# The last columns of one record of each round, loaded in sixteen strided pieces

## The chip, the core and the metric

The kernel runs on one core of a Trainium2 chip. The metric is the time of one execution on the device in microseconds. The kernel before took 724.65 us in the median of three runs (724.24 to 724.74).

The core has a matrix engine (TensorE, PE in the profile), a vector engine (DVE), a scalar engine (ACT), a general engine (POOL, unused here) and a queue that issues transfers (SP). Sixteen DMA engines move the bytes between the chip's memory and the core's SBUF, whose 128 partitions are the rows of every tile below.

## The reference

A decode step of two attention layers and two feed-forward layers, in float32, with one new token for each of 4 sequences:

```
x = x + A(layernorm(x))      # attention, 32 heads of 128, the last 1024 cached positions
x = x + B(layernorm(x))      # relu(x @ w1) @ w2, 640 -> 1728 -> 640
x = x + A(layernorm(x))      # the same weights and caches again
x = x + B(layernorm(x))
```

In `A`, the queries are `x @ wq`; the scores of each head against its own 1024 cached keys go through a softmax; the weighted sum of the cached values goes through `wo`. Every key, value and weight is used for four tokens at most, so the work is nearly all reading: each of the two passes over the attention reads the whole cache.

## The kernel before

The host packs everything that one head needs into a record of 128 rows and 9472 columns (`REC`): the head's part of `wq` in columns 0 to 640, its keys for four sequences up to column 4736 (`V`), its values up to 8832 (`WO`), and its part of `wo` in the last 640. A record is 4736 KB. There are 32, and SBUF holds five at a time, in `slot0` to `slot4`; a further tile, `ring`, holds feed-forward weights and, for a while, parts of records.

There are two rounds, each of 32 records and one feed-forward layer. Round 0 takes the records in the order 0 to 31. Round 1 starts with records 27 to 31, which still lie in the slots, and goes on with 0 to 26 (`order`). So position 20 is record 20 in round 0, which lies in slot 0, and record 15 in round 1, which lies in slot 1.

For one head, PE computes the query (tile `q_ps`), transposes it (`misc`), computes the scores (`sc_ps`), transposes the weights of the softmax (`pt_ps`), sums the values (`o_ps`), transposes the result (`misc`) and adds its projection to `acc`. The heads are interleaved: within one step of the loop, PE takes the scores of record n+1, then the values of record n, then the query of record n+2, then the output projection of record n. The last of these releases the slot of record n.

All loads of records and weights are issued by SP, in one order that is fixed when the program is built: `items` lists them, and `pump` issues the head of the list once its columns of its buffer are no longer in use (`live`, cut down by `done`). On the chip, SP takes the loads strictly in that order. A load whose semaphores aren't there yet holds up all that stand behind it. It waits for PE where it overwrites columns that PE reads.

The completion of a load is told by a semaphore. The program uses eight for the loads (named DMAHW0 to DMAHW7 in the instruction list), in turn: each load takes the next one, and one that takes a semaphore waits first until the load that had it before, eight issues earlier, has landed.

Most records are one load of 128 rows by 9472 columns. The first record, the last three of each round (`ending`), and the records that enter while round 1 begins are cut into pieces. All instructions come out of one helper, so nearly all rows of the profile say L81; the tiles tell them apart.

Of the kernel before, what the change touches and what calls it, by code (L numbers as in the profile page):

```python
# [35 lines left out]
P = 128  # L36
# [8 lines left out]
REC = 2 * D + 8 * W  # L45
# [13 lines left out]
W1_SLOT = [[0, 1], [2], [3], [4]]  # L59
W2_SLOT = [22, 20, 8, 4]  # L60
LATE = 3


IDENT, MEAN, NCON = 0, 128, 256
# [24 lines left out]
def decode_kernel(ctx: ExitStack, tc: tile.TileContext, xf, cst, rec, w1, w2, out):  # L89
    nc = tc.nc  # L90
    pe, dve, act, sp = (InOrder(tc, e) for e in (nc.tensor, nc.vector, nc.scalar, nc.sync))
# [13 lines left out]
    hT = on[:, FD:FD + 4 * NB * B].rearrange("p (t j b) -> p t j b", t=4, j=NB)  # L105
    oTs = sb.tile([P, LATE, B], F32, name="oTs")
    qs = sb.tile([P, DH], F32, name="qs")
# [22 lines left out]
    order = [list(range(H)), list(range(H - NS, H)) + list(range(H - NS))]  # L130
    LAST = H - NS

    def home(h, r):

        return h % NS if not r or h >= LAST else (h - 6 + LAST) % NS

    items = []
    at = {}
    live = []
    buffers = dict(enumerate(slot)) | {"ring": ring}  # L140

    def load(key, src, lo, hi, buf, col):
        items.append((key, src, lo, hi, buf, col))

    def piece(r, h, lo, hi, buf=None, col=None):
        load(("rec", r, h), rec[h], lo, hi, home(h, r) if buf is None else buf, lo if col is None else col)

    def ending(r, hs, late):
        a, b, c = hs[-3:]
        end = WO if late else REC  # L150
        for h, lo, hi in ((a, 0, V), (b, 0, V), (a, V, end), (c, 0, V), (b, V, end), (c, V, V + VH), (c, V + VH, end)):
            piece(r, h, lo, hi)
        if late:
            for h in hs[-3:]:
                piece(r, h, WO, REC)


    hs = order[0]
    piece(0, hs[0], 0, V)
    piece(0, hs[0], V, REC)  # L160
    for h in hs[1:-3]:
        piece(0, h, 0, REC)
    ending(0, hs, True)
    for k, col in enumerate(W1_RING):
        load(("w1", 0), w1, k * FF, k * FF + FF, "ring", col)
    n = 0
    for size, col in W2_RING:
        load(("w2", 0), w2, n * FD, (n + size) * FD, "ring", col)
        n += size
# [13 lines left out]
        piece(1, new[i], 0, V, *((old[i], 0) if i < 5 else ("ring", 0)))  # L183
        piece(1, new[i], V, REC, old[i - 1], V)
    for h in new[6:-3]:
        piece(1, h, 0, REC)
    ending(1, hs, False)
    for blocks in W1_SLOT:
        load(("w1", 1), w1, blocks[0] * FF, (blocks[-1] + 1) * FF, home(LAST + 1, 0), blocks[0] * FF)
# [5 lines left out]
    def pump():  # L195

        while items:
            key, src, lo, hi, buf, col = items[0]
            if any(b == buf and x < col + hi - lo and col < y for b, x, y in live):
                return  # L200
            sp.dma_start(buffers[buf][:, col:col + hi - lo], src[:, lo:hi])
            live.append((buf, col, col + hi - lo))
            at.setdefault(key, []).append((lo, hi, buf, col))
            items.pop(0)
# [11 lines left out]
    def done(key, lo, hi):  # L216

        if key[0] == "rec" and key[1] == 0 and key[2] >= LAST:
            return
        for x, y, buf, col in pieces(key):  # L220
            a, b = col + max(lo, x) - x, col + min(hi, y) - x
            if a < b:
                rest = []
                for bb, u, v in live:
                    if bb != buf or v <= a or b <= u:
                        rest.append((bb, u, v))
                    else:
                        rest += [(bb, p, q) for p, q in ((u, a), (b, v)) if p < q]
                live[:] = rest
        pump()  # L230
# [6 lines left out]
    def center(fill):  # L237

        x = acc[:, :FD]
        dve.tensor_reduce(sums, x, op=OP.add, axis=AX.X)  # L240
        if fill:
            busy(256)
        pe.matmul(misc[:, 0:1], mean_of, sums, start=True, stop=True)
        if fill:
            busy(512)
            busy(256)
        dve.tensor_scalar(xc, x, misc[:, 0:1], None, op0=OP.subtract)
        dve.transpose(xT, xc)
        act.activation(square, xc, AF.Square, accum_out=squares)
        dve.tensor_copy(x_sb, x)  # L250
# [117 lines left out]


    pump()  # L370
    residual()
    for r in range(2):
        hs = order[r]
        late = LATE if r == 0 else 1
        center(r > 0)
# [79 lines left out]
```

## Time and profile before

| | before |
|---|---|
| median of 3 runs | 724.65 us |
| the profiled execution's own time | 724.7 us |
| its span, first to last instruction | 722.9 us |
| bytes moved, mean rate over the span | 304.74 MB, 422 GB/s |
| DMA engines' time taken by the loads' queue (q1) | 98.6% |
| PE busy | 530.8 us, 73% |
| DVE busy | 206.5 us, 29% |
| ACT busy | 90.3 us, 12% |

The page shows the span in 40 slices of 18 us, with the DMA engines' mean busy share in tenths and the rate in GB/s in each. The chain of waits is followed back from the last instruction: each row has its start, its length, and the engine or the transfer that it stood in. A row "DMA slot<-rec" in it is a transfer from its issue to its landing, the time behind earlier transfers included. SPq is the queue that issues the loads; its rows give the time of the issue alone, and its waits are listed apart. In the views by windows, the columns are the stretch, its length, the busy time and number of instructions of PE, weight loads, DVE, ACT and POOL, the granted clock of PE, the busy share of the DMA engines (a packet counted whole where it starts, so it can pass 1) and GB/s.

### The profile page before, as it was taken

Reading aid. Unit: us, or ns where it says so; the run is one execution under the profiler, and the core shown is the slowest. Engines: PE = TensorE matmul, PEld = TensorE weight load, DVE = VectorE, ACT = ScalarE, POOL = GpSimd, SP = SyncE. Lnnn points to the kernel's source line nnn. Section 1 sums busy time; section 2 is a strip of 40 time slices with the busy share of each in tenths; the row PEclk is TensorE's granted clock in tenths of the full one; section 3 lists DMA queues with packets and bytes.
Section 4 is the critical chain, followed back from the end, with each engine's and each line's share of the span. In section 5 each row is a group of like instructions: output and inputs, shape, how many; then the busy total and the mean of one; then the engine's idle time right before and its main releaser. Section 6 shows DMA issues by size and latency. Waiting matters only on the chain.

```text
span 722.9 us, 9922 instructions
## 1 busy us (share of the span) xinstructions
PE 530.8 (73%) x4420; PEld 220.2 (30%) x4420; DVE 206.5 (29%) x541; ACT 90.3 (12%) x154; POOL 0.2 (0%) x4
## 2 busy tenths in 40 slices
PE   0666867668677686868999889776867768586987
PEld 0232322323233232323323333232322323232332
DVE  1222233232232223323421343422223222222430
ACT  0301011010110101101111221201011010101120
POOL 0000000000000000000000000000000000000000
PEclk9978788687787878778999999978788788778999
DMA  9999999999999999999999999999999999999996
GB/s 381 436 435 433 429 432 422 429 431 435 436 433 431 429 429 423 433 435 420 421 401 371 410 426 428 446 431 424 429 432 433 433 433 432 433 431 416 429 419 255
DMA packets 15161, 304.74 MB, mean 422 GB/s; under 512 B 1680, under 2 KB 2064, under 8 KB 5136
## 3 DMA queue, kind: packets, MB, share of 16 engines
q1 hardware_dynamic: 14832, 303.91, 98.6%
q8 instruction: 34, 0.56, 0.3%
q10 hardware_dynamic: 288, 0.21, 0.1%
q14 instruction: 7, 0.06, 0.0%
HBM read 304.04 MB, written 0.08 MB: 421 GB/s over the span
## 4 chain that ended last, share of the span: by engine, by line
DMA 81%; PE 15%; DVE 2%; issue 1%; ACT 0%; SPq 0%; DVEq 0%; ACTq 0%
DMA slot<-rec 76%; DMA slot<-w 3%; PE sc_ps L81 3%; PE misc L81 3%; PE acc L81 3%; PE o_ps L81 3%; DMA ring<-w 2%; PE q_ps L81 2%; PE pt_ps L81 2%; DVE on L81 1%; DVE oTs L81 1%; DVE small L81 0%; ACT prob L81 0%; SPq L81 0%; SPq L78 0%
## 5 line engine op out<-in xcount | busy, mean ns | idle before, releaser
L81 PE MATMUL q_ps<-slot,xT 128*4 128x128 f32 x620 | 46.9, 318 | 138.3 <-DMA slot<-rec 137.3
L81 ACT ACTIVATE prob<-sc_ps,small 128x1024 f32<-128x1024 f32 x64 | 71.3, 1115 | 563.0 <-DVE small L81 555.4
L81 PE MATMUL sc_ps<-slot,qT 128*4 128x512 f32 x992 | 132.7, 657 | 1.8 <-DVE qT L81 1.0
L81 PE MATMUL o_ps<-slot,pT 128*4 128x512 f32 x1014 | 120.5, 592 | 1.8 <-DVE pT L81 0.9
L81 DVE TENSOR_REDUCE small<-sc_ps 128x1 f32<-128x1024 f32 x64 | 78.4, 1225 | 129.4 <-PE sc_ps L81 129.4
L81 PE MATMUL pt_ps<-con,prob 128*128 128x128 f32 x518 | 113.4, 364 | 0.0
L81 PEld LDWEIGHTS pt_ps<-con,prob 128*128 128x128 f32 x518 | 83.9, 189 | 28.3 <-issue 27.4
L81 PEld LDWEIGHTS q_ps<-slot,xT 128*4 128x4 f32 x620 | 20.8, 88 | 193.8 <-DMA slot<-rec 181.3
L81 PE MATMUL misc<-con,on 128*128 128x128 f32 x256 | 54.6, 350 | 9.9 <-DVE on L81 9.9
L81 DVE TENSOR_SCALAR qs<-q_ps,small 128x128 f32<-128x128 f32 x64 | 22.3, 349 | 138.3 <-PE q_ps L81 138.0
L81 DVE COPY pT<-pt_ps 128x16 f32<-128x16 f32 x128 | 22.1, 174 | 123.1 <-PE pt_ps L81 123.1
L81 DVE TENSOR_SCALAR on<-o_ps,small 128x512 f32<-128x512 f32 x64 | 48.0, 751 | 29.2 <-PE o_ps L81 29.2
L81 PEld LDWEIGHTS o_ps<-slot,pT 128*4 128x4 f32 x1014 | 25.5, 87 | 82.8 <-issue 76.4
L81 PE MATMUL acc<-slot,oTs 128*4 128x160 f32 x512 | 38.2, 382 | 16.3 <-DVE oTs L81 16.3
L81 PEld LDWEIGHTS misc<-con,on 128*128 128x128 f32 x256 | 34.6, 171 | 31.9 <-DVE on L81 17.4
L81 PEld LDWEIGHTS sc_ps<-slot,qT 128*4 128x4 f32 x992 | 20.8, 89 | 70.5 <-issue 64.8
L81 PE MATMUL misc<-con,qs 128*128 128x128 f32 x64 | 23.5, 368 | 2.3 <-DVE qs L81 2.1
L81 PE MATMUL sc_ps<-slot,con 128*1 128x512 f32 (+1 forms) x50 | 20.8, 506 | 0.0
L81 DVE TENSOR_REDUCE oTs<-misc 128x4 f32<-128x16 f32 x64 | 11.2, 175 | 33.5 <-PE misc L81 33.5
L81 PEld LDWEIGHTS acc<-slot,oTs 128*4 128x4 f32 x512 | 7.2, 84 | 36.6 <-DVE oTs L81 35.8
L81 DVE TENSOR_REDUCE qT<-misc 128x16 f32<-128x64 f32 x64 | 14.4, 225 | 3.4 <-PE misc L81 2.0
L81 PEld LDWEIGHTS misc<-con,qs 128*128 128x128 f32 x64 | 12.6, 198 | 4.1 <-ACT small L81 2.2
(45 smaller groups left out, 101.7 us busy)
## 6 DMA issues: line engine op xcount, KB each, us to landing
slot<-rec SPq DMA_DIRECT2D x46, 4736.0 KB, 31.1
slot<-rec SPq DMA_DIRECT2D x17, 2368.0 KB, 22.1
slot<-rec SPq DMA_DIRECT2D x5, 1024.0 KB, 31.9
ring<-w SPq DMA_DIRECT2D x5, 864.0 KB, 13.7
slot<-rec SPq DMA_DIRECT2D x2, 2048.0 KB, 41.9
slot<-rec SPq DMA_DIRECT2D x3, 1344.0 KB, 9.0
slot<-w SPq DMA_DIRECT2D x3, 864.0 KB, 31.0
ring<-rec SPq DMA_DIRECT2D x1, 2368.0 KB, 16.2
```

The costliest lines, as they stand in the source:

```text
L81: r = build(*args, **kwargs)
```

## The change

One whole record in each round, at position 20, is loaded in two parts: columns 0 to 8320 in one load of 128 rows as before, and the last 1152 columns (the last 512 of the values and all of the `wo` part) in 16 loads. Load r of the 16 takes the 8 rows r, r+16, r+32 up to r+112, from and to the same rows, so that each moves 8 x 4608 bytes, 36 KB. `pump` issues all 16 one behind the other; they count as one piece for the kernel's own bookkeeping, but each is a load of its own with its own semaphore. The bytes and where they land are the same, and so is the work of the other engines. SP issues 32 loads more.

```diff
+EVEN = [slice(0, P)]
+UNEVEN = [slice(r, P, 16) for r in range(16)]
+SHIFTED = 20
+STRIP = 1152
...
-    def piece(r, h, lo, hi, buf=None, col=None):
-        load(("rec", r, h), rec[h], lo, hi, home(h, r) if buf is None else buf, lo if col is None else col)
+    def piece(r, h, lo, hi, buf=None, col=None, rows=EVEN):
+        load(("rec", r, h), rec[h], lo, hi, home(h, r) if buf is None else buf, lo if col is None else col, rows)
+
+    def whole(r, h):
+        if h == order[r][SHIFTED]:
+            piece(r, h, 0, REC - STRIP)
+            piece(r, h, REC - STRIP, REC, rows=UNEVEN)
+        else:
+            piece(r, h, 0, REC)
...
     for h in hs[1:-3]:
-        piece(0, h, 0, REC)
+        whole(0, h)
...
     for h in new[6:-3]:
-        piece(1, h, 0, REC)
+        whole(1, h)
...
-            key, src, lo, hi, buf, col = items[0]
+            key, src, lo, hi, buf, col, rows = items[0]
...
-            sp.dma_start(buffers[buf][:, col:col + hi - lo], src[:, lo:hi])
+            for p in rows:
+                sp.dma_start(buffers[buf][p, col:col + hi - lo], src[p, lo:hi])
```

More of the change, by code (lines that the diff above doesn't have):

```diff
@@ L140, in decode_kernel, with load @@
     buffers = dict(enumerate(slot)) | {"ring": ring}
-    def load(key, src, lo, hi, buf, col):
-        items.append((key, src, lo, hi, buf, col))
-    def piece(r, h, lo, hi, buf=None, col=None):
-        load(("rec", r, h), rec[h], lo, hi, home(h, r) if buf is None else buf, lo if col is None else col)
+    def load(key, src, lo, hi, buf, col, rows=EVEN):
+        items.append((key, src, lo, hi, buf, col, rows))
+    def piece(r, h, lo, hi, buf=None, col=None, rows=EVEN):
[6 more added lines that the diff above has]
+            piece(r, h, 0, REC)
     def ending(r, hs, late):
```

## The prediction

> **What bounds the kernel now.** I read the page first: the DMA lines, then the chain that ended last.
>
> ```profile
> span 722.9 us, 9922 instructions
> DMA  9999999999999999999999999999999999999996
> GB/s 381 436 435 433 429 432 422 429 431 435 436 433 431 429 429 423 433 435 420 421 401 371 410 426 428 446 431 424 429 432 433 433 433 432 433 431 416 429 419 255
> ...
> DMA 81%; PE 15%; DVE 2%; issue 1%; ACT 0%; SPq 0%; DVEq 0%; ACTq 0%
> ...
> slot<-rec SPq DMA_DIRECT2D x46, 4736.0 KB, 31.1
> ```
>
> All 16 DMA engines are nine tenths busy or more from the first slice to the last but one, and the chain is transfers for 81% of the span. The 46 whole records land 31.1 us (median) after they are issued. The chain of waits in order of time gives the pace around the two places that the change touches:
>
> ```profile
> 176.91 30.69 DMA slot<-rec
> 207.65 0.60 PE q_ps L81 x10
> ...
> 210.23 31.98 DMA slot<-rec
> 242.25 0.84 PE q_ps L81 x10
> ...
> 276.01 0.60 PE q_ps L81 x10
> ...
> 309.65 0.60 PE q_ps L81 x10
> ...
> 550.68 0.60 PE q_ps L81 x10
> ...
> 552.65 31.64 DMA slot<-rec
> 584.34 1.01 PE q_ps L81 x10
> ```
>
> Each row of q_ps is the query of a record that has just landed, and the chain shows every third record. 242.25 to 309.65 is six records, 11.23 us each; 550.68 to 584.34 is three, 11.22 us each. So a record is issued nearly three records ahead of its landing: itself and about two more are queued. The transfer issued at 210.23 is record 20 of round 0, the first that is split: counting three records per step from the start, it follows the release of record 15's slot and lands at 242.2. Of round 1, position 20 is record 15, one before the record issued at 552.65 and landed at 584.3, so it lands near 573.1. Both stand where nothing but the transfers sets the pace, as the windows say:
>
> ```profile
> 200.00:300.00 100.00, 71.67 (x557) 29.76 (x559) 27.82 (x70) 10.85 (x18) 0.00 (x0) 0.80 1.00 430
> 550.00:650.00 100.00, 70.91 (x559) 30.70 (x563) 26.32 (x70) 9.64 (x16) 0.00 (x0) 0.80 1.00 431
> ```
>
> The last columns are the DMA share, 1.00, and GB/s, 430 and 431, or 27 GB/s for one of 16 engines; PE is busy for 72 and 71 us of 100. Time in which the DMA engines have nothing queued is therefore lost for good, and time on PE is not.
>
> **What SP waits for.** The DMA queue's own waits, over the run and then from 328 to 350 us:
>
> ```profile
> SPq L81 <- PE acc L81: 499.0, 52, 26.6
> SPq L81 <- DMA slot<-rec: 68.2, 17, 6.0
> ...
> SPq L81 <- DMA slot<-rec: 16.6, 4, 5.3
> ```
>
> Mostly SP waits for PE to release a slot. But it has also waited 17 times for a landing. These come where round 0's ending is cut in many short loads: a load takes one of eight completion semaphores in turn, and before it is issued, the load eight issues earlier must have landed. With whole records, the load eight back is long done. In the changed kernel's instruction list for SP, the first split record reads (semaphore waited for in brackets):
>
> ```
> L86 DMACopy slot0_70<-rec 128x8320 [waits DMAHW2_49,PE_49]
> L86 DMACopy slot0_70<-rec 8x1152 [waits PE_49]
> L86 DMACopy slot0_70<-rec 8x1152 x2
> L86 DMACopy slot0_70<-rec 8x1152 [waits DMAHW3_49]
> ...
> L86 DMACopy slot0_70<-rec 8x1152 [waits DMAHW7_49]
> L86 DMACopy slot0_70<-rec 8x1152 [waits DMAHW0_49]
> ...
> L86 DMACopy slot0_70<-rec 8x1152 [waits DMAHW7_49]
> L86 DMACopy slot1_71<-rec 128x9472 [waits DMAHW0_49,PE_49]
> ```
>
> Number the sixteen short loads 0 to 15. Loads 0 to 2 go out at once; 3 to 6 wait for records 16 to 19; load 7 waits for the landing of the 8320 columns of its own record; 8 to 15 wait for loads 0 to 7, and record 21 waits for load 8. The same order stands at round 1's split record.
>
> **The change part by part.**
>
> *The shortened load.* 8320 of 9472 columns take 11.24 x 8320/9472 = 9.87 us, so it lands 1.37 us earlier, at about 240.9 us. It needs the slot only up to the first three quarters of the last values, so it can be issued a few us earlier; that is worth nothing, as two records are queued ahead of it.
>
> *The sixteen loads, up to load 7.* Load 7 can't be issued before 240.9, and record 21, which went out about 222 us before (one record after 210.23), is stuck behind it for some 20 us. By then records 18, 19 and the 8320 columns have drained: the queue is empty but for loads 0 to 6, one row of 4608 B to an engine, 4608/27 = 0.17 us each and 1.2 us together. That is a stall of the whole stream, and this is the term that decides. From the last byte of the 8320 columns to full rate on record 21:
>
> ```profile
> 720.44 0.35 SPq L81 DMA_DIRECT2D out<-on  x1
> ...
> out<-on SPq DMA_DIRECT2D x1, 80.0 KB, 1.6
> ```
> ```profile
> 721.25:721.50 0.25, 0.00 (x0) 0.00 (x0) 0.00 (x0) 0.00 (x0) 0.00 (x0) 1.00 0.71 210
> 721.50:721.75 0.25, 0.00 (x0) 0.00 (x0) 0.00 (x0) 0.00 (x0) 0.00 (x0) 1.00 0.41 118
> 721.75:722.00 0.25, 0.00 (x0) 0.00 (x0) 0.00 (x0) 0.00 (x0) 0.00 (x0) 1.00 0.00 0
> ```
>
> 1. Landing: the store of the output is issued at 720.44 and done 1.6 us later, at 722.04; its last bytes move between 721.50 and 721.75. From last byte to semaphore is 0.3 to 0.5 us: 0.4.
>
> ```profile
> 1.16 0.90 SPq L81 DMA_DIRECT2D slot<-rec  x2
> ...
> 1.16 2.73 SPq L81 DMA_DIRECT2D slot<-rec  x5
> ...
> 300.40 0.80 SPq L81 DMA_DIRECT2D slot<-rec  x2
> ...
> 395.53 0.33 SPq L81 DMA_DIRECT2D slot<-rec  x1
> ```
>
> 2. Issues: loads 7 to 15 are nine issues ahead of record 21. SP's rows show loads issued one behind the other: two in 0.80 and 0.90 us, five in 2.73, so 0.40 to 0.55 us each, and 0.33 is one alone. No load of 8 rows is in the trace. The spread is small and nothing in the rows ties the time to a load's size; I take 0.43, so 9 x 0.43 = 3.9 us. The ends: at 0.33 it is 3.0, at 0.55 it is 5.0. Were a short load's issue free, load 15 still waits for load 7's landing, a trip of 1.6 us by the store, and then 1.6 + 0.33 = 1.9.
>
> ```profile
> 395.50:396.00 0.50, 0.50 (x8) 0.00 (x0) 0.00 (x0) 0.00 (x0) 0.00 (x0) 1.00 0.53 221
> 396.00:396.25 0.25, 0.25 (x4) 0.00 (x0) 0.00 (x0) 0.00 (x0) 0.00 (x0) 1.00 0.08 25
> 396.25:396.50 0.25, 0.25 (x5) 0.23 (x2) 0.09 (x1) 0.00 (x0) 0.00 (x0) 1.00 0.51 94
> 396.50:396.75 0.25, 0.25 (x3) 0.08 (x3) 0.25 (x1) 0.00 (x0) 0.00 (x0) 1.00 1.07 164
> 396.75:397.00 0.25, 0.25 (x10) 0.23 (x10) 0.25 (x1) 0.00 (x0) 0.00 (x0) 1.00 1.28 268
> 397.00:397.50 0.50, 0.35 (x10) 0.05 (x1) 0.50 (x1) 0.00 (x0) 0.00 (x0) 1.00 0.52 139
> 397.50:398.00 0.50, 0.05 (x1) 0.05 (x1) 0.40 (x2) 0.27 (x1) 0.00 (x0) 1.00 0.94 383
> ```
>
> 3. Restart: at 395.53 a load is issued into a queue that runs dry. From 396.0 to 398.0 the engines move 399 KB (GB/s by length, summed) where 431 GB/s would be 862: 1.07 us lost, and 0.47 from the issue to 396.0: 1.5 us.
>
> Together 0.4 + 3.9 + 1.5 = 5.8 us without work, in which the strip's bytes move: they were 1.37 us of the stream, which comes off. 4.4 us for a strip, 8.8 us for both.
>
> [...]
>
> *The engines' lag.* A drained queue makes fifteen engines wait for the slowest. How far they part is seen at the end:
>
> ```profile
> 712.00:713.00 1.00, 0.92 (x4) 0.22 (x3) 0.17 (x1) 0.97 (x3) 0.00 (x0) 1.00 0.99 411
> ...
> 715.00:716.00 1.00, 0.37 (x8) 0.02 (x2) 0.00 (x0) 0.00 (x0) 0.00 (x0) 1.00 0.54 223
> ...
> 718.00:719.00 1.00, 0.99 (x30) 0.39 (x20) 0.00 (x0) 0.00 (x0) 0.00 (x0) 1.00 0.08 31
> q8 instruction: 34, 0.56, 0.3%
> ```
>
> The first engines are done near 713, the last at 719. Levelling them is free for the slowest, but a later instruction packet (0.3% of 16 x 722.9 us over 34 packets: 1.0 us) can make another engine the slowest, which its lead would have absorbed. 0 to 1 us for each strip; I take 0.25, so 0.5 in all.
>
> *Consumers.* Record 20's last values and its output projection wait for the strip, but PE takes its values only after the scores of record 21, which lands some 17 us later; were this cover gone, it would be the trip of a load, 1.6 us, once a round. Slots 1 to 3 are free by the time that record 21 goes out, so the queue fills again at once. The added issues outside the stall (loads 0 to 6 of each strip) lie inside SP's waiting.
>
> **Sum.** 724.7 us for the profiled execution (722.9 and 1.8 around it; the median of the runs, 724.65, is the same) + 8.8 + 0.5 = 734.0 us, 1.3% slower.
>
> **The rivals.**
>
> *No drain: the strip only loads half the engines.* If loads 7 to 15 came out in time, the eight rows of a load would lie on eight engines, which would carry 2 x 1.37 us of strip where they carried 1.37: 1.37 more each round, 727.4 us. [...] Against the rival: load 7's wait for its own record's 8320 columns, at a depth of one.
>
> *Faster.* The same, with the slowest engine among the eight that are spared: it drops 1.37 us a round, 722.0 us. For it: near 718 only one engine in sixteen is still at work (0.08), so relief in the right place counts. It decides only if the queue doesn't drain and the slowest leads the loaded eight by over 2.7 us of lag.
>
> *Serial loads.* If each of the nine waited for a round trip, 9 x 1.6 = 14.4 in place of 3.9: 10.5 us more a strip, 755 us. Against: load 8 waits for 0, not for 7.
>
> *Hidden.* If the stream had slack to win back the pause, it would be 724.7; DMA shares of 1.00 speak against it.
>
> **How the numbers follow.** The stall, 0.87, at 734.0; no drain 0.05; faster 0.04; serial 0.03; hidden 0.01. A difference of 0.2% (1.4 us) is what a measurement here can tell. Ends of the stall: issues nearly free give 0.4 + 1.9 + 1.5 - 1.37 = 2.4 a strip, 729.6; issues of 0.55 with the full lag give 5.5 + 1.0 a strip, 737.8. I widen these to 729.0 and 739.0, which leaves out the four rivals and a few hundredths of the stall. Faster 0.04, same 0.02, slower 0.94.
>
> **What would show it.** In the profile after: SP's waits for a landing of slot<-rec grow from 68 us by some 50, those for PE shrink; the DMA share falls to near nothing for 3 to 5 us near 241 and near 577 us; the query of record 21 comes about 4 us later than 253.5 (242.25 + 11.23), and the shift stays to the end; 32 loads of 36 KB. I am wrong if SP passes load 7 before 240 us, or if short loads are issued in much less or more than 0.4 us.

## The result and the profile after

The changed kernel takes 740.67 us (median of 5 runs, 740.46 to 741.46) against 724.65 us: 1.0227 times as long, 95% interval 1.0215 to 1.0238. Forecast were 734.0 us and a range of 729 to 739. The sign and the mechanism came as forecast, but the loss is 16.0 us where 9.3 were forecast, and the time lies outside the range.

The page of the changed kernel, the lines that answer to those of before:

```profile
span 739.7 us, 9962 instructions
...
DMA  9999999999999699999999999999999599999997
GB/s 380 443 430 427 423 430 443 433 425 427 427 435 382 251 426 439 437 428 417 422 410 385 406 427 428 438 429 429 437 429 430 204 441 431 427 425 429 431 416 299
...
DMA 76%; PE 20%; DVE 2%; issue 1%; SPq 0%; ACT 0%; another core or an unknown queue 0%; DVEq 0%; ACTq 0%
```

Two slices, the 14th with 251 GB/s and the 32nd with 204, stand out of a row of about 430, the first with an edge in the 13th (382). The other slices, the last apart, are as before within some 20 GB/s: the loss is in two places. The profiled execution took 741.46 us, its span is 16.8 us longer than that of before.

SP's waits, and then its issues: the second view gives the start of the first issue, the time to the end of the last and their number.

```profile
SPq L86 <- PE acc L86: 427.4, 46, 26.4
SPq L86 <- DMA slot<-rec: 122.2, 23, 11.5
```
```profile
242.24 5.91 SPq L86 DMA_DIRECT2D slot<-rec  x10
```

SP waits 54 us more for landings and 72 us less for PE's projections (acc). The ten issues are loads 7 to 15 and record 21. The last takes 0.38 us, so record 21 goes out at 247.77: 5.53 us after load 7, or 0.61 us for each of nine issues. Around them, windows (busy times, PE's clock, DMA share, GB/s):

```profile
238.00:242.00 4.00, 2.24 (x24) 0.31 (x16) 2.05 (x3) 1.21 (x2) 0.00 (x0) 1.00 0.26 73
242.00:248.00 6.00, 5.47 (x43) 2.95 (x47) 1.10 (x5) 0.00 (x0) 0.00 (x0) 0.72 0.18 51
248.00:250.00 2.00, 2.00 (x24) 0.39 (x16) 1.11 (x1) 0.00 (x0) 0.00 (x0) 1.00 1.09 305
250.00:252.00 2.00, 0.46 (x8) 0.00 (x0) 0.94 (x3) 1.21 (x2) 0.00 (x0) 1.00 0.74 322
```

For ten microseconds the engines move 73 and then 51 GB/s. The query of a record marks its landing; the first row is from the chain, the others from the order in time on PE:

```profile
205.95 36.27 DMA slot<-rec
...
242.26 0.60 PE q_ps L86 x10
```
```profile
261.87 1.02 PE L86 MATMUL q_ps<-slot,xT 128*4 128x128 f32 x10 [11.42 <-DMA slot<-rec]
...
601.09 1.02 PE L86 MATMUL q_ps<-slot,xT 128*4 128x128 f32 x10 [11.60 <-DMA slot<-rec]
```

The row of before that answers to 261.87:

```profile
253.55 1.02 PE L81 MATMUL q_ps<-slot,xT 128*4 128x128 f32 x10 [3.37 <-DMA slot<-rec]
```

Record 21's query comes at 261.87 in place of 253.55, 8.3 us later. The same query in round 1 comes at 601.09 in place of 584.34, 16.75 us later. That is the whole difference of the spans.

### The profile page after: what moved, and what is told of

Same layout as the page of the kernel before. It is cut to its first block, busy times and chain, and to the rows that moved or that the text cites. A ratio compares the mean times of both kernels' runs of the same rounds, so it can differ in the third digit from the quotient of the medians.

```text
span 739.7 us, 9962 instructions
## 1 busy us (share of the span) xinstructions
PE 532.4 (72%) x4420; PEld 220.4 (30%) x4420; DVE 206.5 (28%) x541; ACT 90.4 (12%) x154; POOL 0.2 (0%) x4
## 4 chain that ended last, share of the span: by engine, by line
DMA 76%; PE 20%; DVE 2%; issue 1%; SPq 0%; ACT 0%; another core or an unknown queue 0%; DVEq 0%; ACTq 0%
DMA slot<-rec 72%; PE sc_ps L86 5%; PE o_ps L86 4%; PE misc L86 3%; PE pt_ps L86 3%; PE acc L86 3%; DMA slot<-w 3%; PE q_ps L86 2%; DVE on L86 1%; DMA ring<-w 1%; DVE oTs L86 1%; DVE small L86 0%; ACT prob L86 0%; SPq L86 0%
```

## The experiments

My theory was the prediction's: the sixteen loads use up the eight semaphores, SP can't issue record 21 until the 8320 columns have landed, and the transfers run dry. The rivals were that the split itself costs, that the strip's bytes cost because they lie on part of the engines, that each short load costs for itself, and that which rows a load takes matters. Each kernel was timed beside the kernel before, which took 724.23 us (median) beside the first four, 724.07 beside the next four and 724.72 beside the last three.

**Two loads.** The split without the sixteen loads.

```diff
-UNEVEN = [slice(r, P, 16) for r in range(16)]
+UNEVEN = [slice(0, P)]
```

> The same record in two loads, 8320 and 1152 columns, both of 128 rows. Theory (the sixteen loads use up the eight semaphores, SP is held until the 8320 columns have landed, and the transfers run dry): record 21 waits only for record 17 here, nothing runs dry, and the time is that of before, 724.7 us within 0.7. Rival (the split record itself, or the strip's late landing, holds up PE): 728 us or more.

Measured: 724.50 us, ratio 1.0005 (0.9995 to 1.0014). The split costs nothing.

**Half the bytes.** Sixteen loads of 8 rows, but 640 columns.

```diff
-STRIP = 1152
+STRIP = 640
```

> Sixteen loads of 8 rows as in the changed kernel, but of 640 columns, so 56% of the bytes. Theory: the pause is made of issues and not of bytes; the strip's bytes that move inside it are worth 0.6 us a round less, so about 742 us (741 to 743). Rival (bytes on part of the engines): 56% of 16 us, about 733.6 us.

Measured: 741.25 us, 1.0232 (1.0216 to 1.0247). With 56% of the bytes the loss is as large. The bytes don't make it.

**Eight loads.**

```diff
-UNEVEN = [slice(r, P, 16) for r in range(16)]
+UNEVEN = [slice(r, P, 8) for r in range(8)]
```

> The strip as eight loads of 16 rows, 8 apart. Theory: load 7 still waits for the 8320 columns and record 21 for load 0, but one issue lies between where nine did, eight times 0.61 us less a round: 16.0 - 2 x 4.9 = 6.2 us over before, about 730.9 us (729 to 733). Rival (8 rows a load, on part of the engines, are the cause): 724.7 to 727 us.

Measured: 732.33 us, 1.0112 (1.0096 to 1.0129), half of the loss. Record 21 is issued 0.59 us after load 7 (243.00 and 243.59), as expected. But the chain of this kernel shows the 8320 columns late:

```profile
205.26 37.73 DMA slot<-rec
242.99 0.04 issue
```

They land at 242.99, where 240.9 was expected. In the changed kernel they landed at 242.22, no earlier than the whole record of before. So a second thing is at work, before the pause.

**Four loads, 40 + 40 + 40 + 8 rows.** No load waits for its own record, and each goes over a part of the engines: as they land, the semaphores of the loads of 40 rows take ten steps and that of the load of 8 rows takes eight.

```diff
-UNEVEN = [slice(r, P, 16) for r in range(16)]
+UNEVEN = [slice(0, 40), slice(40, 80), slice(80, 120), slice(120, P)]
```

> The strip as four loads, three of 40 rows and one of 8, so few that no load waits for its own record. Theory: the transfers don't run dry, and the strip costs at most 1.4 us a round more on the engines that carry it: 722 to 727.5 us. Rival (the cost is the strip's bytes on part of the engines, whatever the number of loads): near the 740.7 us of the changed kernel, above 735.

Measured: 731.28 us, 1.009 (1.0071 to 1.011): between the two, so both expectations fell. SP's waits for landings are as before (69.7 us, 17), and nothing runs dry; the windows show something else:

```profile
236.00:240.00 4.00, 4.00 (x33) 0.75 (x32) 1.35 (x3) 0.00 (x0) 0.00 (x0) 0.81 1.10 336
240.00:244.00 4.00, 1.50 (x18) 0.70 (x14) 1.22 (x4) 1.21 (x2) 0.00 (x0) 1.00 1.03 256
```

The engines are busy throughout (1.10 and 1.03), and move only 336 and 256 GB/s. In the trace, a packet of 4608 bytes takes 0.18 us at first and then around 0.34, and record 21's packets beside them about 2.5 us in place of 1.40. It looks as if they were in each other's way; the next two runs try that.

**Four loads of 32 rows, spread or together.** The same number of loads, of rows and of bytes; only which rows differs.

```diff
-UNEVEN = [slice(r, P, 16) for r in range(16)]
+UNEVEN = [slice(r, P, 4) for r in range(4)]                  # spread
...
+UNEVEN = [slice(32 * r, 32 * r + 32) for r in range(4)]      # together
```

> The strip as four loads of 32 rows, 4 apart. No load waits for its own record. Theory (neither a pause nor rows in each other's way): the time of before, 724.5 us within 1. Rival (four short loads cost 3.5 us a round as with 40, 40, 40 and 8 rows, by their number): 731 us.

> The strip as four loads of 32 rows that lie together. [...] Rival (which rows makes no difference): the same as with 32 rows 4 apart.

Measured: spread 724.58 us, 1.0005 (0.9996 to 1.0014), no cost; together 730.64 us, 1.0084 (1.0067 to 1.0101), 6.6 us. The same window, spread and then together:

```profile
240.00:244.00 4.00, 2.96 (x39) 1.89 (x39) 1.64 (x6) 1.03 (x2) 0.00 (x0) 1.00 1.09 469
```
```profile
240.00:244.00 4.00, 0.20 (x8) 0.14 (x9) 0.00 (x0) 0.00 (x0) 0.00 (x0) 0.69 0.89 230
```

Neither number nor bytes, but the choice of rows decides between 469 and 230 GB/s. Spread came as expected; the rival for together, that the rows make no difference, is refuted: 724.58 and 730.64 us. Half the rate for the strip alone would, by estimate, cost once more the 1.37 us that its bytes take in the stream, 1.4 us a round, and the run shows 3.3. The chain shows where most of it comes from, spread and then together:

```profile
205.68 35.18 DMA slot<-rec
240.85 0.04 issue
```
```profile
204.25 39.51 DMA slot<-rec
243.76 0.04 issue
```

The 8320 columns, which are issued ahead of the strip, land 2.9 us later when the strip's rows lie together; their last packets take up to 2.2 us in place of 1.23. So the strip slows the load ahead of it too. What a packet waited for, no trace shows.

**Sixteen loads by columns.** All rows, all engines, the same waits.

```diff
-            for p in rows:
-                sp.dma_start(buffers[buf][p, col:col + hi - lo], src[p, lo:hi])
+            if rows is UNEVEN:
+                for c in range(0, hi - lo, 72):
+                    sp.dma_start(buffers[buf][:, col + c:col + c + 72], src[:, lo + c:lo + c + 72])
+            else:
+                sp.dma_start(buffers[buf][:, col:col + hi - lo], src[:, lo:hi])
```

> The strip as sixteen loads of all 128 rows, 72 columns each: the same number of loads and the same waits, but each on all sixteen engines and with no choice of rows. Theory (the pause as predicted, with issues of 0.43 us; the rest of the loss comes from loads of 8 rows: a slower issue, 0.61 us, and slow writes): 732 to 736 us. Rival (sixteen loads with these waits cost 8 us a round, whatever their shape): 740.7 us within 1.

Measured: 738.05 us, 1.0187 (1.0172 to 1.0202): above the theory's 736, below the rival's 739.7.

```profile
241.01 5.36 SPq L86 DMA_DIRECT2D slot<-rec  x10
```
```profile
259.94 1.01 PE L86 MATMUL q_ps<-slot,xT 128*4 128x128 f32 x10 [10.97 <-DMA slot<-rec]
```

Load 7 goes out at 241.01, where the prediction had it: with all rows in a load, the 8320 columns land in time. Ten issues take 5.36 us; record 21's, the last, starts 4.98 after the first. That is 0.55 us each in the mean, but eight of the nine steps take 0.37 to 0.53 us, 0.46 in the mean, and one takes 1.29, because a single issue lasts 1.19 us; why it does is open. In round 1 no step stands out:

```profile
578.44 4.60 SPq L86 DMA_DIRECT2D slot<-rec  x10
```

The last of these ten takes 0.38, so the nine take 4.22 us, 0.47 each, near the 0.43 of the prediction. From record 21's issue to its query pass 13.95 us in round 0 and 14.35 in round 1, where 13.1 were forecast (1.5 + 11.24 + 0.4). In the profiled execution this kernel pays 6.4 and 6.3 us for its two strips where 4.4 were forecast: the excess is mostly this restart and, in round 0, the one long step.

**Sixteen loads of 8 rows, 4 apart.**

```diff
-UNEVEN = [slice(r, P, 16) for r in range(16)]
+UNEVEN = [slice(b + r, b + 32, 4) for b in range(0, P, 32) for r in range(4)]
```

> Sixteen loads of 8 rows as in the changed kernel, but with the 8 rows 4 apart inside blocks of 32 in place of 16 apart over all 128. Theory (rows 16 apart get in each other's way and in that of the load ahead, whose last packets take up to 2 us in place of 1.23): the 8320 columns land about 1.4 us earlier each round, about 738 us (737 to 739.5). Rival (which rows makes no difference): 740.7 us within 0.7.

Measured: 740.05 us, 1.0217 (1.0202 to 1.0232), over the theory's range and inside the rival's. By the time alone, which rows a load takes would make no difference; the landing shows that it does:

```profile
204.40 36.48 DMA slot<-rec
...
240.92 0.60 PE q_ps L86 x10
```
```profile
240.89 6.45 SPq L86 DMA_DIRECT2D slot<-rec  x10
```

The 8320 columns land at 240.87 in place of 242.22: the late landing was a matter of rows. But of the 1.35 us gained, 0.55 are lost again, for the issues take longer, 6.08 us from load 7 to record 21 in place of 5.53. The rest, 0.8 us a round, is more than the medians show: 740.05 and 740.67 us, each 16.0 us over the kernel before beside it.

**Six and seven loads by columns.** The edit is that of the sixteen loads by columns, with widths of 192 and 165.

> The strip as six loads of all 128 rows, 192 columns each. Record 21 then takes the semaphore that record 19 had, so it is issued when record 19 lands, with the 8320 columns still to move. Theory (the loss is the run-dry transfers, and begins when record 21 has to wait for its predecessor's own 8320 columns): the time of before, 724.3 us within 1. Rival (each short load costs by itself, evenly from the first): six sixteenths of what sixteen such loads cost, 14.0 us, so about 729.5 us.

> As with six, but seven loads of 165 columns (the last 162). Record 21 now takes the semaphore of the 8320 columns and can't be issued before they have landed. Theory: a step between six and seven: landing 0.4 us and restart 2.4 us less the strip's 1.4 us, 1.4 us a round over before, 727.0 us (726 to 728.5). Rival (each short load costs by itself): 730.2 us, 0.9 us over six loads.

Measured: six 725.74 us, 1.0018 (1.0008 to 1.0027); seven 727.54 us, 1.0039 (1.0024 to 1.0054). The same window, six and then seven:

```profile
240.00:244.00 4.00, 3.12 (x39) 1.89 (x39) 1.67 (x6) 1.15 (x2) 0.00 (x0) 1.00 1.17 483
```
```profile
240.00:244.00 4.00, 2.80 (x27) 1.83 (x28) 0.85 (x3) 0.40 (x2) 0.00 (x0) 0.81 0.70 218
```

With six loads the engines don't stop; with the seventh, the first that puts record 21 on the 8320 columns' semaphore, they fall to 0.70 and 218 GB/s. The step is 1.8 us, 0.9 a round; 1.4 a round over before was expected, and 2.8/2 = 1.4 was found. The 1.0 us of six loads is over the range expected (724.3 within 1). An estimate from the packets explains part of it: a packet of 768 bytes takes 0.036 us, 48 of them on an engine 1.73 us, where eight of 4608 bytes at 0.18 take 1.44. That is 0.3 a round, 0.6 in all, the lower end of the interval.

**Round 0 only.**

```diff
-        if h == order[r][SHIFTED]:
+        if r == 0 and h == order[r][SHIFTED]:
```

> The changed kernel with the split in round 0 alone. Theory: each split costs the same and nothing of it is won back before the end, so half of the 16.0 us: 732.3 us (731.5 to 733.2). Rival (a pause in round 0 is partly won back around the feed-forward layer, where PE sets the pace): below 731 us.

Measured: 733.04 us, 1.0116 (1.0099 to 1.0133): 8.3 us, half of the whole.

No version here beats the kernel before.

## Why the prediction was right and wrong

**Right: what bounds the kernel, and the mechanism.** The stream of transfers was the only bound, SP was held at load 7 until the record's own 8320 columns had landed, and the transfers ran dry twice. The two loads, the six and seven loads and the half strip show it from three sides. (One reading was too narrow: of the 68.2 us of SP's waits for landings in the kernel before, 28.6 lie at round 0's ending; 25.7 lie behind 650 us, at round 1's, and 11.4 at the start. The forecast doesn't rest on it.) The loss stayed to the end, PE and the slots absorbed none of it, and each round paid the same.

**Wrong: the size of the pause, 4.4 us a strip forecast and 8.3 found.** Record 21's query in round 0, by the prediction's own terms:

| term | forecast | measured | more |
|---|---|---|---|
| the 8320 columns land | 240.9 | 242.2 | 1.3 |
| nine issues, loads 7 to 15 | 3.9 | 5.5 | 1.6 |
| from record 21's issue to its query (restart 1.5 + 11.24 + landing 0.4) | 13.1 | 14.1 | 1.0 |

1. *The shortened load* was to land 1.37 us earlier. It landed no earlier, because loads 0 to 6 were taken for harmless: "4608/27 = 0.17 us each and 1.2 us together". Their rows, 16 apart, slowed each other (0.18 to 0.35 us a packet) and the last packets of the load ahead, which took up to 2.1 us in place of 1.23. The share of that load which landed last, at 242.2, seems to lie on an engine without any of the strip: all eight shares of load 0, which was issued behind it, had landed at 240.94. So an engine's own share of the strip was not what held it up. With rows 4 apart, and with all rows in each load, the landing came at 240.9. So the credit for the strip's bytes was spent before the pause began.

2. *Issues.* I took 0.43 us from loads of 128 rows, and wrote that nothing tied the time to a load's size. A load of 8 rows is issued in 0.61 us when they lie 16 apart and in 0.68 when they lie 4 apart, above the upper end of 0.55 too; the prediction had named that as a sign of being wrong. What decided in these runs is whether the rows lie apart. The issues alone in ns (least, median, most; a single whole record takes about 330): loads 7 to 15 of the changed kernel; the four loads of 40 and 8 rows; 32 rows together; 32 rows spread:

```profile
L86 SPq DMA_DIRECT2D slot<-rec x9: 563/563/564, 242.2 to 247.1; - x9
```
```profile
L86 SPq DMA_DIRECT2D slot<-rec x4: 295/314/353, 210.6 to 211.7; - x4
```
```profile
L86 SPq DMA_DIRECT2D slot<-rec x4: 341/415/421, 210.5 to 211.9; - x4
```
```profile
L86 SPq DMA_DIRECT2D slot<-rec x4: 537/587/594, 209.3 to 211.2; - x4
```

The last two have the same number of rows and bytes, and differ by 0.17 us. In the changed kernel's trace a load of 8 rows moves in eight packets of 4608 bytes; its semaphore takes one step about 1.0 us after the issue begins (load 7: 242.24, 243.22) and then eight as they land, where that of 128 rows takes sixteen. A small number of steps is not what makes an issue long: the loads of 40 and 8 neighbouring rows, whose semaphores take ten and eight as they land, are issued fastest. What SP does in the longer issue, no trace shows.

3. *Restart.* 1.5 us came from a place (395.5) where the engines had not all stopped. After the pause, fifteen of the sixteen first packets of record 21 take 1.5 to 2.6 us in place of 1.40, as the kernel's first packets do at its start (1.0 to 1.9 us in place of 0.71, for half the bytes); 2.5 us would have been the term. From the issue of record 21 (247.77) to its first packet (248.77) 1.0 us passed. Why the first packets are slow is open.

*The engines' lag* was forecast at 0.5 us and measured at about none: from record 21's query in round 1 to the end, the delay stays at 16.8.

**The rivals.** Faster and hidden are refuted by the time itself, serial loads by load 8, which went out 0.61 us after load 7 and not a round trip later. "No drain" did not happen here, but its price was wrong as well. Where the transfers don't run dry, four loads of 40 and 8 rows on ten and eight engines cost 3.5 us a round and not 1.37, and four loads of 32 neighbouring rows cost 3.3 where as many rows 4 apart cost nothing, so most of that goes with which rows a load takes and not with an uneven share. How much of it lies in the changed kernel's loss, beyond the 1.3 us of the late landing, was not tried.

## What to carry to other kernels

Count the semaphores before a load is cut into pieces: with eight in turn, the load that comes eight issues after another can't go out before that one has landed (load 7 went out at 242.24, when the 8320 columns had landed at 242.22), and in a stream that is bound by its transfers a chain of short loads drains the queue: from 242 to 248 us the engines moved 51 GB/s, where before they had moved 423. Six pieces of all 128 rows cost 1.0 us here, sixteen pieces of 8 rows 16.0. If a load must be cut by rows, let its rows lie 4 apart (32 rows 4 apart cost nothing, 32 together 6.6 us). Spreading them over all 128 is not enough: behind 8 rows 4 apart the load ahead landed in time, behind 8 rows 16 apart 1.3 us late and behind 16 rows 8 apart 2.1 (round 0). And rows that lie apart take SP longer to issue, 0.6 to 0.7 us each against 0.34 to 0.47 for 32 or 40 neighbouring rows.

## What the runs showed of the hardware beyond that

- DMA engines can be fully busy and slow: 256 GB/s at a share of 1.03, where the spread rows give 469 at 1.09.
- What an issue costs SP goes mostly by whether its rows lie apart, and hardly by their number or the bytes: 0.6 to 0.7 us from one issue to the next for 8 to 32 rows that lie apart, 0.34 to 0.47 for 32 or 40 neighbouring rows, and 0.47 in the mean for all 128 rows of 288 bytes.
- After a complete stop, record 21 needs 14.1 us from its issue to its query, where 11.24 us is its share of a running stream: 2.9 us more, by estimate 2.5 of restart with the 0.4 that the prediction read off the store for the landing.
